# Filling the remainder of the MLP's gate and up contraction with zero rows to 128

## The chip, the cores and the metric

The kernel runs on one core of one Trainium2 chip, as one program. TensorE (PE in the profile, its weight loads apart as PEld) multiplies, VectorE (DVE), ScalarE (ACT) and GpSimd (POOL) do the elementwise work, and DMAs are issued from the queues of SyncE (SP) and ScalarE. The metric is the device time of one execution in microseconds (us); the time of a kernel is the median of several executions.

## The reference

One transformer block with adaptive layer norm: six modulation rows come from a conditioning vector, attention runs over a cached window of 512 keys, and a gated MLP follows. Sequence 2048, model width D = 576, 32 query and 16 key heads of 128, MLP width F = 4608, all float32.

```python
mod = (_silu(c) @ w_mod).reshape(c.shape[0], 6, 1, -1)
sa, ca, ga, sb, cb, gb = (mod[:, i] for i in range(6))
h = _layernorm(x) * (1 + ca) + sa
x = x + ga * _A_ref(h, A_k_cache, A_v_cache, A_wq, A_wo)   # attention
h = _layernorm(x) * (1 + cb) + sb
gate = jnp.einsum("bsd,df->bsf", h, W_gate)                # contraction over D = 576
up = jnp.einsum("bsd,df->bsf", h, W_up)                    # the same
gate = gate * (gate > 0)
x = x + gb * jnp.einsum("bsf,fd->bsd", gate * up, W_down)
```

## The kernel before

*Exact products from rounded parts.* Matrix operands are cut into a rounded high part and the difference as a low part (type float32r), and a product is high x high, low weight x high, and high weight x low: three matmuls that add up in one PSUM tile.

*The MLP's two contractions* (gate and up, side by side) are done as a Winograd form of Strassen's scheme: both operands are cut into 2 x 2 blocks, and seven products P1 to P7 of sums of blocks replace eight. The contraction of 576 is halved by this into 288 = 128 + 128 + 32. So one half has two full tiles of 128 rows (t = 0 and 1), each with a high and a low tile, and a remainder of 32 rows (t = 2). The remainder's three partial products are laid one above the other in the rows of one tile: the weights hold low, high, high in rows 0 to 95, the activations hold high, high, low. One matmul of 96 rows then does what three would. One product of one half (`prod`, line 967) is therefore seven matmuls: three for t = 0, three for t = 1, and the remainder at line 976. There are 36 steps m of seven products, gate and up each, so 504 products.

*Where the activations come from.* The layer norm of the MLP's input writes its transposed rows to DRAM (`hb_store`, line 240): four tiles of 128 rows for each block qb of 512 tokens, and a tile `hb[qb, 4]` of 2 x 3 x 32 rows, where each of the two halves' 32 remaining rows is stored three times. `hb_load` (line 250) reads them back. The sums of blocks that the products need (`B11`, `T2`, ...) are made by VectorE for the first half of the tokens (`h0_comb`, `h0_hi`, `h0_cut`, lines 844 to 874) and by GpSimd for the second (`h_later`, line 796, during the first half of the MLP), cut into high and low, and parked in DRAM tiles `hkeep` until `h_back` (line 877) loads them for the MLP half that uses them. In the profile these are the tiles h, hx, hy, hz, hk and hop.

*Where the weights come from.* In the first half (m = 0 to 17) raw tiles are loaded (`wr`), summed by VectorE (`w_sums`, line 783), and cut into `wop` by ScalarE and GpSimd (lines 753 to 755), and each `wop` is stored to DRAM (`wk`); the second half loads it from there. A raw weight tile has 128 rows for t = 2 already, four copies of its 32 rows.

*What sets the order.* TensorE, VectorE, ScalarE and GpSimd follow the order in which the code is written out: in attention a list of steps, each with a due time (`step(name, t, fn)`, t = 10 per unit of attention), in the MLP the slots of each product. Beside the products TensorE runs the down projection of the step before (`md`, line 632), which VectorE adds to the residual (line 643). SP's queue takes its DMAs in the order of the same code and holds at the first one whose buffer is not free. A DMA also waits for the transfer that last used its completion counter, of which there are eight.

Of the kernel before, what the change touches and what calls it, by code (L numbers as in the profile page):

```python
# [7 lines left out]
F32 = mybir.dt.float32  # L8
# [25 lines left out]
def kernel(  # L34
# [177 lines left out]
    def prep_out(d, k, src, key, slot=None, at=(None, "wC")):  # L212
# [11 lines left out]
        def cut():  # L224
# [9 lines left out]

    hT = [None] * NQB

    hb = {(qb, d): dr.tile([2, 3, 32, 512] if d == 4 else [P, 512], F32, name=f"hb{qb}_{d}")
          for qb in range(NQB) for d in range(5)}

    def hb_store(qb, d, cols, f, eng=None):  # L240
        eng = eng or nc.sync
        if d < 4:
            eng.dma_start(hb[qb, d][:, cols], f)
            return
        for j in range(2):
            s = f[32 * j:32 * j + 32]
            eng.dma_start(hb[qb, 4][j, :, :, cols].rearrange("r p n -> p r n"),
                              s[:, None, :].to_broadcast([32, 3, s.shape[1]]))

    def hb_load(dst, qb, j, t):  # L250
        if t < 2:
            nc.sync.dma_start(dst, hb[qb, 2 * j + t])
        else:
            nc.sync.dma_start(dst[:96], hb[qb, 4][j].rearrange("r p n -> (r p) n"))

    h0, late = {}, []
    pend, pend_act = [], []
# [516 lines left out]
    def w_sums(m, s):  # L774

        r = {ij: wraw.get((m, *ij)) for ij in RAW}
        if s == "S2":
# [8 lines left out]

    TERMS = {"B11": "+00", "B21": "+10", "T2": "+11-01+00", "T3": "+11-01", "T1": "+01-00",
             "T4": "+10-11+01-00", "B22": "+11"}
    hkeep = {(b, s, k): dr.tile([96 if k == 2 else P, 512], F32R, name=f"hk{b}_{s}_{k}")
             for b in range(2) for s in TERMS for k in range(5)}  # L790

    def terms_of(s, table):
# [3 lines left out]
    def h_later(b, s, t):  # L796

        st = {}
        n = 96 if t == 2 else P
        terms = terms_of(s, TERMS)  # L800

        def get(dst, j, k):
            hb_load(dst, 2 * b + k, j, t)

        def begin():
            if b:
                ab = wp.tile([P, 2, 512], F32, tag="wC", name=f"hx{b}_{s}_{t}")
                st["a"], st["b"] = ab[:, 0, :], ab[:, 1, :]
            else:
                for x in "ab":  # L810
                    st[x] = hp.tile([P, 512], F32, tag="hT", name=f"h{x}{b}_{s}_{t}")
            for x, term in zip("ab", terms):
                get(st[x], *term[1:])

        def comb(i):
            x, y = st["a"][:n], st["b"][:n]
            nc.gpsimd.tensor_tensor(x, x, y, op=ALU.add if terms[i][0] == "+" else ALU.subtract)
            if i + 1 < len(terms):
                get(st["b"], *terms[i + 1][1:])

        def cut():
            a = st["a"]
            hi = hp.tile([P, 512], F32R, tag="hT", name=f"hy{b}_{s}_{t}")
            nc.scalar.copy(hi[:n], a[:n])
            if t < 2:
                lo = st["b"].bitcast(F32R)
                nc.gpsimd.tensor_sub(lo, a, hi.bitcast(F32))
                stores.append((hkeep[b, s, 3 + t], lo))
            else:
                nc.gpsimd.tensor_sub(hi[64:96], a[64:96], hi[64:96].bitcast(F32))  # L830
            stores.append((hkeep[b, s, t], hi[:n]))

        return [begin] + [lambda i=i: comb(i) for i in range(1, len(terms))] + [cut]
# [8 lines left out]
        hb_load(h0[j, k, t], k, j, t)  # L842

    def h0_comb(dst, a, b, op, t):
        n = 96 if t == 2 else P
        nc.vector.tensor_tensor(h0[(*dst, t)][:n], h0[(*a, t)][:n], h0[(*b, t)][:n], op=op)

    hy0 = {}

    def h0_hi(s, x, t):  # L850
        a, n = h0[(*x, t)], 96 if t == 2 else P
        hi = hy0[s, t] = hp.tile([P, 512], F32R, tag="hT", name=f"hy0_{s}_{t}")
        nc.scalar.copy(hi[:n], a[:n])

# [4 lines left out]
            h0_cut(s, H0_CUT[s], t, True)  # L859

    def h0_cut(s, x, t, stay=False):
        a, n = h0[(*x, t)], 96 if t == 2 else P
        hi = hy0[s, t]
        if t < 2:
            lo = hy0[s, 3 + t] = hp.tile([P, 512], F32R, tag="hT", name=f"hz0_{s}_{t}")
            nc.gpsimd.tensor_sub(lo, a, hi.bitcast(F32))
        else:
            nc.vector.tensor_sub(hi[64:96], a[64:96], hi[64:96].bitcast(F32))
        if stay:
            if t == 2:  # L870
                hop[0, s] = [hy0[s, k] for k in range(5)]
            return
        if t < 2:
            stores.append((hkeep[0, s, 3 + t], lo))
        stores.append((hkeep[0, s, t], hi[:n]))

    def h_back(b, s):
        hs = hop[b, s] = [hp.tile([P, 512], F32R, tag="hT", name=f"hop{b}_{s}_{k}") for k in range(5)]
        for k in range(5):
            nc.sync.dma_start(hs[k][:96 if k == 2 else P].bitcast(F32), hkeep[b, s, k].bitcast(F32))  # L880


    WTERMS = {"P1": "+00", "P2": "+01", "P6": "+10+11-00", "P7": "+00-10", "P5": "+10+11", "P4": "+11",
# [83 lines left out]
    def prod(m, s, n, xx):  # L967
# [3 lines left out]
        ops = []  # L971
        for t in range(2):
            ops += [(w[:, xx, t, :], hs[t]), (w[:, xx, 3 + t, :], hs[t]), (w[:, xx, t, :], hs[3 + t])]
        ops.append((w[0:96, xx, 2, :], hs[2][0:96]))
        for i, (a, c) in enumerate(ops):
            nc.tensor.matmul(ps, a, c, start=s not in heir(m) and i == 0 and s not in seeds_of(m), stop=i == len(ops) - 1,  # L976
                             skip_group_check=True)
# [268 lines left out]
    def step(name, t, fn, *args):  # L1246
        sched.append((t + PLAN.get(name, 0), len(sched), fn, args))
# [151 lines left out]
    step("m3.col", 250, setd(mods, "b0", lambda: mod_col(3, 0.0)()))  # L1399
    step("m4.col", 400, setd(mods, "b", lambda: (mods["b0"], mod_col(4, 1.0)())))  # L1400

    mkeep = dr.tile([P, D], F32, name="mkeep")

    def m5_back():
# [317 lines left out]
```

## Time and profile before

| | us |
|---|---|
| median of three executions | 2897.92 (2895.86 to 2900.04) |
| the profiled execution | 2898.73 |
| its span, first to last instruction | 2895.9 |
| attention and what precedes it | 0 to about 1614 |
| first half of the MLP, with the weights' preparation | about 1614 to 2258 |
| second half of the MLP | about 2258 to 2896 |
| mean granted clock of TensorE in the span | 0.996 |

A line of a group reads: source line, engine, operation, output<-inputs by the program's names, shape and count, then busy time in us, mean duration of one in ns, and after the second bar the idle time of the engine just before them with what ended it. For a matmul, 128*128 or 96*128 are the rows and columns of the array that it uses. Matmuls overlap: each begins while the one before is still draining, so the distance between two starts says how long one holds the array, and its duration is longer than that. Lines of the timeline give start (us), duration (us) and the merged instructions; idle time before them stands in brackets.

### The profile page before, as it was taken

What the parts mean: (1) busy time and instruction counts of PE and PEld (TensorE: products, weight loads), DVE (VectorE), ACT (ScalarE), POOL (GpSimd) and SP (SyncE); (2) the same over time, 40 slices, a digit from 0 to 9 for tenths busy, and PEclk for the clock granted to TensorE, in tenths of its full rate; (3) what the DMA queues carried; (4) which work ended last, traced back from release to release, by engine and by line L of the source; (5) the groups of instructions that cost most, each with busy time, mean ns of one, the idle gap of its engine ahead of it and who ended that gap; (6) DMA issues with size and microseconds to landing.
All of it is one profiled execution on the core that took longest, in us unless ns stands there. A gap on an engine that the chain in (4) does not pass through costs nothing.

```text
span 2895.9 us, 41262 instructions
## 1 busy us (share of the span) xinstructions
PE 2852.8 (99%) x15214; PEld 2485.6 (86%) x15214; DVE 2145.8 (74%) x2967; ACT 1496.0 (52%) x2105; POOL 2115.4 (73%) x1564
## 2 busy tenths in 40 slices
PE   6999999999999999999999999999999999999999
PEld 5788888888888888888888888888888888888888
DVE  7778888888878888777889755676676466666666
ACT  5666666666676666666756444443444122222221
POOL 5688888888888889776778766777777256555553
PEclk9999999999999999999999999999999999999999
DMA  4012222222233223222244456666667954444442
GB/s 160 26 42 71 71 96 82 78 87 97 93 93 97 91 66 131 97 74 78 66 149 134 146 211 224 228 235 221 227 229 261 327 163 151 150 152 160 152 152 105
DMA packets 162697, 396.43 MB, mean 137 GB/s; under 512 B 14912, under 2 KB 61760, under 8 KB 162496
## 3 DMA queue, kind: packets, MB, share of 16 engines
q1 hardware_dynamic: 131472, 282.15, 30.4%
q10 hardware_dynamic: 31024, 111.65, 9.8%
q8 instruction: 120, 1.97, 0.3%
q14 instruction: 81, 0.66, 0.1%
HBM read 268.73 MB, written 153.32 MB: 146 GB/s over the span
## 4 chain that ended last, share of the span: by engine, by line
PE 91%; POOL 3%; DVE 3%; ACT 2%; issue 1%; DMA 1%; SPq 0%; ACTq 0%; POOLq 0%; DVEq 0%
PE gu L976 26%; PE wo L632 13%; PE qps L418 13%; PE md L632 8%; PE st_P L1078 6%; PE s L491 4%; PE s L490 4%; PE s L492 4%; PE pv L607 4%; PE pv L606 4%; PE pv L605 4%; PE qm L518 1%; POOL lo L572 1%; ACT p L565 0%; DVE ws L783 0%
## 5 line engine op out<-in xcount | busy, mean ns | idle before, releaser
L572 POOL TENSOR_TENSOR lo<-p,hi 128x1024 fp32r<-128x1024 f32 x256 | 608.8, 2401 | 1.1 <-ACT hi L552 1.1
L581 POOL TENSOR_TENSOR ks<-ks,p 128x512 f32<-128x512 f32 x256 | 343.7, 1342 | 270.5 <-ACT p L565 213.0
L495 DVE TRANSPOSE_TENSOR_REDUCE t<-s 128x32 f32<-128x1024 f32 x256 | 316.7, 1244 | 136.7 <-PE s L492 125.5
L976 PE MATMUL gu<-hop_B,wop 128*128 128x512 f32 (+1 forms) x1512 | 378.9, 394 | 0.1
L976 PEld LDWEIGHTS gu<-hop_B,wop 128*128 128x128 f32 (+1 forms) x1512 | 276.1, 188 | 52.7 <-ACT lflh L961 0.9
L976 PE MATMUL gu<-hop_T,wop 128*128 128x512 f32 (+1 forms) x1260 | 319.9, 393 | 0.0
L418 PE MATMUL qps<-hTa,wA 128*128 128x512 f32 x1288 | 311.2, 392 | 4.4 <-DVE hTa L366 2.1
L632 PE MATMUL wo<-woga,ohi 128*128 128x288 f32 x1472 | 306.7, 301 | 0.0
L563 DVE TENSOR_TENSOR p<-s,mb 128x1024 f32<-128x1024 f32 x246 | 290.3, 1219 | 4.1
L418 PEld LDWEIGHTS qps<-hTa,wA 128*128 128x128 f32 x1288 | 242.7, 189 | 57.4 <-DVE hTa L366 4.2
L552 ACT CAST hi<-p 128x1024 fp32r<-128x1024 f32 x256 | 269.2, 1052 | 7.1
L632 PE MATMUL md<-wogb,hhi 128*128 128x288 f32 x1280 | 262.2, 297 | 3.5 <-DVE acc L643 2.5
L565 ACT ACTIVATE p<-p 128x1024 f32<-128x1024 f32 x246 | 259.9, 1056 | 7.6 <-DVE p L563 7.4
L976 PEld LDWEIGHTS gu<-hop_T,wop 128*128 128x128 f32 (+1 forms) x1260 | 228.4, 188 | 41.0
L470 ACT ACTIVATE qhi<-qps 128x512 fp32r<-128x512 f32 x128 | 76.5, 597 | 340.4 <-PE qps L418 340.4
L643 DVE TENSOR_TENSOR acc<-md,acc 128x576 f32<-128x576 f32 x160 | 120.8, 755 | 169.3 <-PE md L632 168.9
L632 PEld LDWEIGHTS wo<-woga,ohi 128*128 128x128 f32 x1472 | 239.3, 189 | 7.3
L632 PEld LDWEIGHTS md<-wogb,hhi 128*128 128x128 f32 x1280 | 214.0, 189 | 16.6 <-DVE acc L643 4.0
L1087 DVE TENSOR_TENSOR acc<-st_P,acc 128x576 f32<-128x576 f32 x160 | 121.1, 757 | 133.8 <-PE st_P L1078 133.8
L632 PE MATMUL wo<-woga,olo 128*128 128x288 f32 x736 | 217.5, 295 | 0.4 <-POOL olo L621 0.3
L632 PE MATMUL md<-wogb,hlo 128*128 128x288 f32 x640 | 189.5, 296 | 0.0
L641 ACT COPY acc<-wo 128x576 f32<-128x576 f32 x233 | 148.2, 636 | 66.8 <-PE wo L632 61.6
(274 smaller groups left out, 7111.5 us busy)
## 6 DMA issues: line engine op xcount, KB each, us to landing
wop<-wk_P SPq DMA_DIRECT2D x133, 640.0 KB
wk_P<-wop ACTq DMA_DIRECT2D x119, 640.0 KB
wr<-wlay SPq DMA_DIRECT2D x68, 384.0 KB
rogb<-wd SPq DMA_DIRECT2D x68, 288.0 KB
againq<-akq SPq DMA_DIRECT2D x18, 640.0 KB
rwA<-wq SPq DMA_DIRECT2D x32, 320.0 KB
wlay<-wg SPq DMA_DIRECT2D x36, 256.0 KB
roga<-wo SPq DMA_DIRECT2D x32, 288.0 KB
```

Of the source, the lines that this page charges most:

```text
L418: return [lambda i=i, a=a, b=b: nc.tensor.matmul(ps, a, b, start=(i == 0), stop=(i == n - 1)) for i, (a, b) in enumerate(ops)]
L495: nc.vector.tensor_reduce(t4[u][:, 2 * h:2 * h + 2, :].rearrange("p k b -> p (k b)"), t.rearrange("p k (b j) -> p (k b) j", j=32), axis=AX ...
L552: nc.scalar.copy(hi_[u, h], pt[u, h])
L563: nc.vector.tensor_tensor(p, t, bc[u][:, None, :].to_broadcast([P, 2, 512]), op=ALU.subtract)
L565: nc.scalar.activation(p, p, AF.Exp, bias=0.0, scale=1.0)
L572: nc.gpsimd.tensor_sub(lo_[u, h], pt[u, h], hi_[u, h].bitcast(F32))
L581: nc.gpsimd.tensor_tensor(ks_[u], ks_[u], p[:, j, :], op=ALU.add)
L632: nc.tensor.matmul(ps[:, half, :H2], a[:, sl], w[b][:, cs], start=(n == 0 and seed is None), stop=(n == 5), skip_group_check=seed is not None)
L641: nc.scalar.copy(av, ps[:, :, :H2])
L976: nc.tensor.matmul(ps, a, c, start=s not in heir(m) and i == 0 and s not in seeds_of(m), stop=i == len(ops) - 1, skip_group_check=True)
L1078: nc.tensor.matmul(ps[:, j, :H2], x[:, sl], w[:, y, :], start=n == 0 and not second, stop=n == 2, skip_group_check=True)
L1087: nc.vector.tensor_tensor(t, ps[:, :, :H2], t, op=ALU.add)
```

## The change

The DRAM tile of the remainder gets a fourth row of blocks, `[2, 4, 32, 512]`, of zeros. A new step `hb.r` in attention (due at 300, before unit 30) fills it with eight DMAs of 32 x 512 from a part of `wmod` that the host has padded with zeros. Everything that touched 96 rows of the third activation tile now takes 128: its loads, the sums, the cast to the high part, the park in `hkeep`, and the reload; the subtraction that makes the low part stays on rows 64 to 95. The remainder's matmul uses all 128 rows of weights and activations; weight rows 96 to 127, a fourth copy of the high part, meet zeros.

```diff
-    hb = {(qb, d): dr.tile([2, 3, 32, 512] if d == 4 else [P, 512], F32, name=f"hb{qb}_{d}")
+    hb = {(qb, d): dr.tile([2, 4, 32, 512] if d == 4 else [P, 512], F32, name=f"hb{qb}_{d}")
...
-            eng.dma_start(hb[qb, 4][j, :, :, cols].rearrange("r p n -> p r n"),
+            eng.dma_start(hb[qb, 4][j, 0:3, :, cols].rearrange("r p n -> p r n"),
                               s[:, None, :].to_broadcast([32, 3, s.shape[1]]))
+
+    def hb_rest():
+        for qb in range(NQB):
+            for j in range(2):
+                nc.sync.dma_start(hb[qb, 4][j, 3], wmod[0, 64:96, 4 * D:4 * D + 512])
...
-            nc.sync.dma_start(dst[:96], hb[qb, 4][j].rearrange("r p n -> (r p) n"))
+            nc.sync.dma_start(dst, hb[qb, 4][j].rearrange("r p n -> (r p) n"))
...
-    hkeep = {(b, s, k): dr.tile([96 if k == 2 else P, 512], F32R, name=f"hk{b}_{s}_{k}")
+    hkeep = {(b, s, k): dr.tile([P, 512], F32R, name=f"hk{b}_{s}_{k}")
...
-        n = 96 if t == 2 else P
+        n = P
...
-            nc.sync.dma_start(hs[k][:96 if k == 2 else P].bitcast(F32), hkeep[b, s, k].bitcast(F32))
+            nc.sync.dma_start(hs[k].bitcast(F32), hkeep[b, s, k].bitcast(F32))
...
-        ops.append((w[0:96, xx, 2, :], hs[2][0:96]))
+        ops.append((w[:, xx, 2, :], hs[2]))
...
+    step("hb.r", 300, hb_rest)
```

The line `n = 96 if t == 2 else P` becomes `n = P` in `h_later`, `h0_comb`, `h0_hi` and `h0_cut` alike.

On SP's queue the eight new DMAs come into the attention phase, between the load of a tile of wq (`rwA`) and copies into the weights' DRAM layout (`wlay`); `wm` is a modulation tile, `rkv` keys. Before:

```order
L203 DMA rkv_0_4326<-kv 128x512
L1418 DMA wlay<-wu 2x128x256
L189 DMA rwA_4419<-wq 128x640
L1418 DMA wlay<-wu 2x128x256
L137 DMA wm_2_4544<-wmod 128x576
L1418 DMA wlay<-wg 2x128x256
```

With the change:

```order
L189 DMA rwA_4419<-wq 128x640
L253 DMA hb_4_142<-wmod 32x512 x2
L253 DMA hb_4_147<-wmod 32x512 x2
L253 DMA hb_4_152<-wmod 32x512 x2
L253 DMA hb_4_157<-wmod 32x512 x2
L1424 DMA wlay<-wu 2x128x256
L137 DMA wm_2_4552<-wmod 128x576
```

The copies and loads that followed `rwA` now stand behind eight more DMAs. Nothing else moves on this queue, and the other engines keep their order instruction by instruction.

Where the first half of the MLP hands over to the second, SP reloads the activations of the second half (`hop`, the third tile ends in `_2`) between the first weights of that half (`wop`). Before:

```order
L768 DMA wop_22812<-wk_P_159 128x1280
L880 DMA hop_T_0_22814<-hk_T_0_377 128x512
L880 DMA hop_T_1_22815<-hk_T_1_378 128x512
L880 DMA hop_T_2_22816<-hk_T_2_379 96x512
L880 DMA hop_T_3_22817<-hk_T_3_380 128x512
L880 DMA hop_T_4_22818<-hk_T_4_381 128x512
L768 DMA wop_22856<-wk_P_161 128x1280
```

With the change:

```order
L773 DMA wop_22820<-wk_P_159 128x1280
L885 DMA hop_T_0_22822<-hk_T_0_377 128x512
L885 DMA hop_T_1_22823<-hk_T_1_378 128x512
L885 DMA hop_T_2_22824<-hk_T_2_379 128x512
L885 DMA hop_T_3_22825<-hk_T_3_380 128x512
L885 DMA hop_T_4_22826<-hk_T_4_381 128x512
L773 DMA wop_22864<-wk_P_161 128x1280
```

The order is the same; each third tile carries 128 rows in place of 96.

More of the change, by code (lines that the diff above doesn't have):

```diff
@@ L844, in h0_comb @@
     def h0_comb(dst, a, b, op, t):
-        n = 96 if t == 2 else P
+        n = P
         nc.vector.tensor_tensor(h0[(*dst, t)][:n], h0[(*a, t)][:n], h0[(*b, t)][:n], op=op)
@@ L850, in h0_hi @@
     def h0_hi(s, x, t):
-        a, n = h0[(*x, t)], 96 if t == 2 else P
+        a, n = h0[(*x, t)], P
         hi = hy0[s, t] = hp.tile([P, 512], F32R, tag="hT", name=f"hy0_{s}_{t}")
@@ L861, in h0_cut @@
     def h0_cut(s, x, t, stay=False):
-        a, n = h0[(*x, t)], 96 if t == 2 else P
+        a, n = h0[(*x, t)], P
         hi = hy0[s, t]
```

## The prediction

> **What bounds the kernel now.** I read the page's busy shares first, then its chain of waits.
>
> ```profile
> span 2895.9 us, 41262 instructions
> PE 2852.8 (99%) x15214; PEld 2485.6 (86%) x15214; DVE 2145.8 (74%) x2967; ACT 1496.0 (52%) x2105; POOL 2115.4 (73%) x1564
> PE 91%; POOL 3%; DVE 3%; ACT 2%; issue 1%; DMA 1%; SPq 0%; ACTq 0%; POOLq 0%; DVEq 0%
> ```
>
> TensorE is the bound: 99% busy, and 91% of the chain. The other engines' time counts only where TensorE waits for it, so the next view is the MLP by stages (us, then busy us of PE, PEld, DVE, ACT and POOL, granted clock, DMA share, GB/s).
>
> ```profile
> 1614.00:2258.00 644.00, 641.37 (x3520) 565.20 (x3520) 418.82 (x408) 277.79 (x388) 474.10 (x411) 1.00 0.63 225
> 2258.00:2882.00 624.00, 622.95 (x3348) 545.03 (x3346) 394.44 (x547) 146.08 (x272) 338.69 (x331) 1.00 0.50 164
> 2240.00:2260.00 20.00, 20.00 (x112) 17.68 (x111) 10.03 (x9) 7.01 (x10) 13.06 (x11) 1.00 0.96 339
> 2260.00:2280.00 20.00, 19.93 (x110) 17.32 (x109) 8.94 (x12) 2.26 (x3) 2.57 (x2) 1.00 1.04 394
> 2280.00:2300.00 20.00, 20.00 (x109) 17.55 (x108) 10.51 (x15) 2.45 (x4) 3.90 (x3) 1.00 1.00 366
> ```
>
> In both halves TensorE has about 1 to 3 us of idle time to give back. So the change can gain only by making matmuls shorter, or by touching one of the few stalls. The DMA engines are half busy in general, but full from about 2240 to 2300, where the first half hands over to the second.
>
> **The matmuls that change.** One product is seven matmuls; its last is the 96-row remainder. The groups of that line, shapes kept apart (count, busy us, mean ns of one, idle before):
>
> ```profile
> L976 PE MATMUL gu<-hop_B,wop 128*128 128x512 f32 x1296 | 334.6, 393 | 0.1
> L976 PE MATMUL gu<-hz_T,wop 128*128 128x512 f32 x216 | 84.2, 390 | 0.0
> L976 PE MATMUL gu<-hop_B,wop 96*128 96x512 f32 x216 | 85.3, 395 | 0.0
> L976 PE MATMUL gu<-hop_T,wop 96*128 96x512 f32 x180 | 71.1, 395 | 0.0
> L976 PE MATMUL gu<-hy_T,wop 96*128 96x512 f32 x108 | 42.6, 395 | 0.0
> L976 PEld LDWEIGHTS gu<-hop_B,wop 128*128 128x128 f32 x1296 | 235.6, 188 | 43.7 <-ACT lflh L961 0.9 <-issue 0.5
> L976 PEld LDWEIGHTS gu<-hop_B,wop 96*128 96x128 f32 x216 | 40.6, 188 | 9.0
> ```
>
> There are 216 + 180 + 108 = 504 remainders. The weight loads are the same, 188 ns either way. The matmul itself is never shorter with fewer rows: 395 ns for 96, 390 to 393 for 128. So no work is added by the zero rows on TensorE, and there may be 2 to 5 ns to gain on each. Busy times overlap, so the bound on the gain is taken from the distances between starts (start us, duration us):
>
> ```profile
> 2001.15 0.39 PE L976 MATMUL gu<-hz_T,wop 128*128 128x512 f32 x1
> 2001.38 0.62 PE L976 MATMUL gu<-hy_T,wop 128*128 128x512 f32 x2
> 2001.84 0.39 PE L976 MATMUL gu<-hz_T,wop 128*128 128x512 f32 x1
> 2002.06 0.40 PE L976 MATMUL gu<-hy_T,wop 96*128 96x512 f32 x1
> 2002.29 0.43 PE L632 MATMUL md<-wogb,hhi 128*128 128x288 f32 x2
> ```
>
> A full-row matmul holds the array for 0.23 (2001.15 to 2001.38) or 0.22 us (2001.84 to 2002.06), the remainder for 0.23 (2002.06 to 2002.29). No gap of a whole switch is visible; what is there is at most 0.01 us, the grain of the view.
>
> *Term 1, 504 remainders at 128 rows.* Lower end 0 (0.23 against 0.23). Upper end 504 x 10 ns = 5.0 us of gain. No loss, since no full-row group of this line is above 395 ns. I take the mean of the two duration differences, 395 - 393 = 2 and 395 - 390 = 5, so 3.5 ns: **-1.8 us**.
>
> A rule speaks against even this. The Trainium skill, "TensorE: Matmul & The Clock Gate", section "Why this matters for your kernels", has a single matmul of K = 32 take the time of one with K = 128, so row count would be free in both directions. By that rule term 1 is 0 and the time is that of the first rival below. The trace agrees as far as 96 rows are no faster than 128; the extra 2 ns the rule leaves unexplained.
>
> *Term 2, casts, sums and subtractions on 128 instead of 96 rows.* The shapes stand side by side:
>
> ```profile
> L817 POOL TENSOR_TENSOR hx_T<-hx_T 128x512 f32<-128x512 f32 x14 | 18.0, 1285 | 1.7 <-DMA hx_T<-hb 1.5 <-DMA rogb<-wd 0.2
> L817 POOL TENSOR_TENSOR hx_T<-hx_T 96x512 f32<-96x512 f32 x7 | 9.0, 1285 | 2.2 <-DMA hx_T<-hb 2.2
> L824 ACT CAST hy_T<-hx_T 128x512 fp32r<-128x512 f32 x8 | 4.9, 618 | 2.5 <-POOL hx_T L817 2.5
> L824 ACT CAST hy_T<-hx_T 96x512 fp32r<-96x512 f32 x4 | 2.5, 618 | 1.8 <-POOL hx_T L817 1.7
> ```
>
> 1285 against 1285 ns, 618 against 618: rows cost nothing there. The four DVE sums of line 846 I put with them. **0 us**; even 5 ns on each of these 7 + 7 + 7 + 4 instructions would be 0.1 us.
>
> *Term 3, eight small DMAs on SP in the attention phase.* They stand between the load of a wq tile and the next weight copy on SP's queue:
>
> ```profile
> 414.52 0.33 SPq L189 DMA_DIRECT2D rwA<-wq  x1
> 414.89 0.58 SPq L1418 DMA_DIRECT2D wlay<-wu  x1
> 422.50 0.34 SPq L137 DMA_DIRECT2D wm<-wmod  x1
> ```
>
> At 0.33 to 0.58 us an issue, eight take 2.6 to 4.6 us. The copy at 414.89 behind them is not wanted before the MLP, and the next load that an engine waits for goes out at 422.50, after 7.0 us in which SP only waits. **0 us**; without that cover the wm load would be 4.6 us late, and DVE's modulation step after it.
>
> *Term 4, bytes.* Every transfer of the third tile grows from 192 to 256 KB: 18 loads (hx, h), 11 stores and 11 reloads (hk), 40 x 64 KB = 2.6 MB. At 63% DMA share this is hidden. In the full stretch it is not:
>
> ```profile
> 2245.86 4.39 SPq L880 DMA_DIRECT2D hop_B<-hk_B  x5
> 2254.62 3.91 SPq L768 DMA_DIRECT2D wop<-wk_P  x3
> 2260.43 5.28 PE L976 MATMUL gu<-hop_B,wop 128*128 128x512 f32 x21
> 2295.99 4.99 PE L976 MATMUL gu<-hop_B,wop 128*128 128x512 f32 x21
> ```
>
> Five reloads need 4.39 us to issue where one needs 0.33: SP is held by its own earlier transfers. Behind them stand the first wop loads of the second half, and 21 matmuls that begin at 2260.43 take 5.28 us where the same 21 take 4.99 later. So TensorE already waits some 0.3 us here, and the slack is nil. 64 KB (65.5 kB) at about 380 GB/s are 0.17 us; two enlarged reloads lie just ahead of that wop load (0.35 us), seven in the whole stretch (1.2 us). Lower end 0, if the extra rows travel beside the others; upper end 1.2 us. I take the middle, **+0.6 us**.
>
> Here too a rule differs. The Trainium skill, "SBUF — State Buffer", section "Door 1: The DMA port swizzle", puts partitions 96 to 127 on the same ports as 64 to 95, so a 96-row transfer leaves half of the ports half loaded, and the 32 rows would fill them for free. By it the term is 0 and the sum -1.8. No row here shows how long one 96-row load takes against one of 128.
>
> *Sum:* -1.8 + 0 + 0 + 0.6 = **-1.2 us**. The profiled execution took 2898.73 us (its span of 2895.9 and 2.8 around it), 0.8 above the median of 2897.92; so it would be 2897.5 there, and the median **2896.7 us**.
>
> **The rivals.**
>
> *TensorE gains nothing (0 ns on each remainder), the bytes stay:* 2897.92 + 0.6 = 2898.5 us. For it: the 0.23 against 0.23 us of the starts. Against it: three groups, 504 records, all at 395 ns.
>
> *Faster, because a stall goes.* There is one real stall in the MLP (idle time in brackets, then the chain around it):
>
> ```profile
> 2002.82 6.06 DVE L783 TENSOR_TENSOR wr<-wr,wr 128x768 f32<-128x768 f32 x1
> 2006.90:2009.60 2.70, 0.37 (x2) 0.00 (x0) 2.70 (x3) 0.00 (x0) 2.70 (x3) 1.00 1.00 401
> 2009.60 0.68 PE L632 MATMUL md<-wogb,hhi 128*128 128x288 f32 x2 [2.34 <-DVE acc L643]
> 2009.60 3.08 PE md L632 x12
> 2012.68 5.24 PE gu L976 x21
> 2017.92 1.60 PE md L632 x12
> 2048.39 4.83 PE gu L976 x21
> 2009.60:2013.20 3.60, 3.60 (x14) 3.50 (x15) 1.89 (x3) 1.45 (x2) 2.73 (x4) 0.53 0.62 211
> L783 DVE TENSOR_TENSOR wr<-wr,wr 128x768 f32<-128x768 f32 x17 | 21.2, 1248 | 0.0
> ```
>
> A DVE sum that means 1.25 us takes 6.06 while POOL, whose busy time is the fifth of the window's, has no break (2.70 of 2.70 us). The accumulation behind it (line 643) frees the PSUM tile late, TensorE idles 2.34 us, and then has a granted clock of 0.53 for 3.6 us: 3.08 - 1.60 + 5.24 - 4.83 = 1.9 us more. One such stall costs 4.2 us. It depends on which of DVE and POOL starts first, which a shift of a few tenths can turn. If it goes: -1.8 - 4.2 + 0.6 = -5.4, or 2892.5 us; with 5 ns on each remainder 2891.8, with the 10 ns bound 2889.3. Against it: nothing in the change is aimed there, and one in 68 such sums (four lists of 17) came out so.
>
> *Slower, by the same mechanism the other way.* The hx loads release POOL's combinations (line 817 waited for a DMA above), and 64 KB more in each moves POOL's row of work against DVE's sums. From the point where a sum is held over 3 us longer, TensorE idles and the clock drops, at 4.2 us each. Two stalls more than before: -1.8 + 0.6 + 8.4 = +7.2, or 2905.1 us. For it: DVE's four sums per step have little room in some steps, as 6.06 shows. Against it: 67 of 68 passed without harm, at the same durations on POOL.
>
> That the change does not do what it says can be left aside: the remainders' row count is in the instruction, and the profile will print it.
>
> **How the numbers follow.** The forecast, two small terms and as many stalls as before (2896.7): 0.46. TensorE gains nothing (2898.5): 0.18. A stall goes: 0.20; 0.14 of it are beyond the bound that follows, for which some 5 ns on a remainder must come with it (2891.8 to 2889.3), and 0.06 are not (2892.5). More stalls (2905.1): 0.16. About 0.2% of the median, 5.8 us, is what a measurement of this kernel can tell from no change, so faster means below 2892.1 and slower above 2903.7. Faster 0.14, within 0.2% 0.46 + 0.18 + 0.06 = 0.70, slower 0.16. The range for 8 times in 10 reaches from 2891.0, inside the case without the stall, to 2903.3, one stall more than before with the upper byte price and no gain on TensorE (2897.92 + 4.2 + 1.2).
>
> **What would show it.** The remainders appear as 128*128 with a mean of 390 to 393 ns in place of 395 (term 1; 395 again means the first rival). Lines 817 and 824 keep 1285 and 618 ns on 128 rows (term 2). The wm load still goes out near 422.5 us (term 3). The 21 matmuls near 2260 take more than 5.28 us (term 4; 5.28 or less means the rows travel for free). TensorE's waits list 2.3 us on line 643, none, or several of them: that decides between the rivals of both signs. The forecast is wrong if the first or the second MLP half differs by more than 3 us without such a wait.

## The result, and the profile after

The changed kernel takes 2884.07 us (median of six executions, 2881.82 to 2885.10), the kernel before beside it on the same chip 2896.15 (2894.11 to 2900.04). The ratio is 0.9956, with a 95% interval of 0.9943 to 0.9969: 12.1 us faster, and by the interval between 9.0 and 16.5. The forecast was 2896.7 with a range down to 2891.0, so the gain was put at a tenth of what it is. The profiled execution took 2884.48 us, its span 2882.7.

The page of the changed kernel, span and busy shares:

```profile
span 2882.7 us, 41271 instructions
PE 2839.4 (98%) x15214; PEld 2476.9 (86%) x15214; DVE 2149.1 (75%) x2967; ACT 1496.2 (52%) x2105; POOL 2115.0 (73%) x1564
```

TensorE ran the same 15214 matmuls in 13.4 us less busy time (2852.8 before) and its weight loads in 8.7 less (2485.6 before); no other engine's time moved by more than 3.3 us. So the time came out of the matmuls, not out of waits. The windows of the changed kernel by stage say where (columns as in the prediction):

```profile
1614.00:2258.00 644.00, 641.12 (x3545) 564.44 (x3543) 425.21 (x411) 280.00 (x391) 476.30 (x414) 1.00 0.64 231
2258.00:2882.00 624.00, 619.78 (x3396) 546.76 (x3396) 399.86 (x555) 144.37 (x269) 337.48 (x330) 1.00 0.48 166
2240.00:2260.00 20.00, 19.80 (x108) 17.13 (x107) 12.18 (x12) 5.73 (x8) 11.65 (x10) 1.00 0.99 372
2260.00:2280.00 20.00, 20.00 (x115) 17.82 (x114) 7.20 (x10) 2.26 (x3) 2.57 (x2) 1.00 1.04 406
2280.00:2300.00 20.00, 20.00 (x111) 17.65 (x110) 9.61 (x14) 3.46 (x5) 6.20 (x5) 1.00 0.92 333
2300.00:2850.00 550.00, 550.00 (x2994) 484.28 (x2994) 358.95 (x499) 136.20 (x257) 324.15 (x320) 1.00 0.46 155
```

The last stretch lies in the second half of the MLP and is the cleanest measure in this study, because nothing waits in it. The same stretch of the kernel before:

```profile
2300.00:2850.00 550.00, 550.00 (x2950) 481.12 (x2949) 353.50 (x491) 135.91 (x256) 322.75 (x319) 1.00 0.48 154
```

In both TensorE is busy for all of the 550 us, at a granted clock of 1.00. Before it gets 2950 matmuls through, after 2994: 44 more, 1.5%. 44 of 2994 in 550 us are 8.1 us. Nearly all products of this half are followed by six matmuls of its other work (`st_P`, 288 columns), 13 in all; 2994 / 13 = 230 products, so each with its six became 35 ns shorter. From the first matmul of a half to its last (the distance of two starts in the trace) the second half shrank by 8.9 us, from 614.1 to 605.2, and the first by 4.8, from 646.8 to 642.0.

The groups of the changed line in the changed kernel:

```profile
L981 PE MATMUL gu<-hop_B,wop 128*128 128x512 f32 x1512 | 374.5, 391 | 0.2 <-DMA wop<-wk_P 0.2
L981 PE MATMUL gu<-hop_T,wop 128*128 128x512 f32 x1260 | 316.0, 391 | 0.0
L981 PE MATMUL gu<-hy_T,wop 128*128 128x512 f32 x540 | 174.2, 392 | 0.2 <-POOL wop L760 0.2
L981 PE MATMUL gu<-hz_T,wop 128*128 128x512 f32 x216 | 84.8, 392 | 0.0
```

All 3528 matmuls are 128*128 now, at means of 391 to 392 ns; before they were 390 to 395. By the mean duration alone the change looks worth 3 to 4 ns on each remainder, as forecast. The starts tell more. Starts of neighbouring products in the second half, on TensorE's timeline of the kernel before:

```profile
2600.32 1.79 PE L976 MATMUL gu<-hop_B,wop 128*128 128x512 f32 x7
...
2602.75 1.79 PE L976 MATMUL gu<-hop_B,wop 128*128 128x512 f32 x7
```

And of the changed kernel:

```profile
2601.04 1.75 PE L981 MATMUL gu<-hop_T,wop 128*128 128x512 f32 x7
...
2603.43 1.76 PE L981 MATMUL gu<-hop_T,wop 128*128 128x512 f32 x7
```

One product and its six take 2.43 us before (2600.32 to 2602.75) and 2.39 after (2601.04 to 2603.43). That is 0.04 us, of which the remainder's own 3 to 4 ns are a small part. Where the rest sits is in the single records of TensorE: the mean distance in ns from each start to the next in this unit, by place, over the 223 products of the second half that six such matmuls follow.

| | 1st | 2nd | 3rd | 4th | 5th | 6th | 7th, the remainder | the six behind | in all |
|---|---|---|---|---|---|---|---|---|---|
| before | 234.7 | 230.8 | 235.4 | 228.2 | 232.0 | 230.6 | 232.5 | 806.8 | 2431.1 |
| changed | 232.4 | 230.7 | 226.7 | 226.7 | 226.7 | 226.7 | 226.7 | 796.4 | 2393.0 |

Of the 38 ns the remainder itself has 5.8, the six behind it 10, and the third to sixth matmul of the product 19, though these start nine to twelve places behind the last remainder.

The stall of the prediction's second rival did not go. On the changed kernel's timeline, VectorE's held sum and TensorE behind it:

```profile
2000.89 6.07 DVE L788 TENSOR_TENSOR wr<-wr,wr 128x768 f32<-128x768 f32 x1
...
2007.68 0.53 PE L637 MATMUL md<-wogb,hhi 128*128 128x288 f32 x2 [2.41 <-DVE acc L648]
...
2009.38 3.84 PE L981 MATMUL gu<-hop_B,wop 128*128 128x512 f32 x16
```

6.07 us for the sum and 2.41 us of idle TensorE, as before (6.06 and 2.34). Only the lowered clock behind it is missing this time: the twelve `md` matmuls take 1.70 us (2007.68 to 2009.38) where they took 3.08.

### The profile page after: what moved, and what is told of

Same layout as the page of the kernel before. It is cut to its first block, busy times and chain, and to the rows that moved or that the text cites. A ratio compares the mean times of both kernels' runs of the same rounds, so it can differ in the third digit from the quotient of the medians.

```text
span 2882.7 us, 41271 instructions
## 1 busy us (share of the span) xinstructions
PE 2839.4 (98%) x15214; PEld 2476.9 (86%) x15214; DVE 2149.1 (75%) x2967; ACT 1496.2 (52%) x2105; POOL 2115.0 (73%) x1564
## 4 chain that ended last, share of the span: by engine, by line
PE 90%; POOL 3%; DVE 2%; ACT 2%; DMA 2%; issue 1%; SPq 0%; ACTq 0%; POOLq 0%; DVEq 0%
PE gu L981 26%; PE wo L637 13%; PE qps L423 13%; PE md L637 8%; PE st_P L1083 6%; PE s L497 4%; PE s L496 4%; PE s L495 4%; PE pv L612 4%; PE pv L611 4%; PE pv L610 4%; PE qm L523 1%; POOL lo L577 1%; ACT p L570 0%; DVE ws L788 0%
## 5 line engine op out<-in xcount | busy, mean ns | idle before, releaser
L981 PE MATMUL gu<-hop_B,wop 128*128 128x512 f32 x1512 | 374.5, 391 | 0.2 <-DMA wop<-wk_P 0.2
L981 PEld LDWEIGHTS gu<-hop_B,wop 128*128 128x128 f32 x1512 | 275.0, 188 | 50.5 <-ACT lflh L966 0.9
L981 PE MATMUL gu<-hop_T,wop 128*128 128x512 f32 x1260 | 316.0, 391 | 0.0
L981 PEld LDWEIGHTS gu<-hop_T,wop 128*128 128x128 f32 x1260 | 227.8, 188 | 38.9
```

## The experiments

Eleven kernels, in the order of the questions. The table has the main figure of the first eight: matmuls in the busy stretch from 2300 to 2850 us, and the ratio of the time to that of the kernel before with its interval. The kernel before was measured again beside each: it took 2896.15 us beside the changed kernel, 2899.02 beside e1 to e4 and 2898.23 beside e5, e6, e9 and e10. So kernels are compared by their ratios rather than by their medians.

| kernel | rows of the seven matmuls | median us | ratio to before | matmuls in 550 us |
|---|---|---|---|---|
| before | 128 x 6, 96 | 2896.15 | | 2950 |
| changed | 128 x 7 | 2884.07 | 0.9956 (0.9943 to 0.9969) | 2994 |
| e1_mm96 | 128 x 6, 96, all data as changed | 2896.49 | 0.9994 (0.9985 to 1.0004) | 2947 |
| e4_copies | 128 x 7, copies for zeros | 2884.91 | 0.9955 (0.9938 to 0.9972) | 2991 |
| e3_all96 | 96 x 7 | 2889.40 | 0.9970 (0.9957 to 0.9983) | 2992 |
| e5_alt96 | 96 at places 2, 4 and 7 | 2897.92 | 0.9995 (0.9986 to 1.0005) | 2959 |
| e9_two96 | 96 at places 6 and 7 | 2896.11 | 0.9986 (0.9976 to 0.9996) | 2961 |
| e10_mid96 | remainder (96) at place 4 | 2896.20 | 0.9993 (0.9982 to 1.0004) | 2958 |
| e6_second96 | 96 in the second half alone | 2894.12 | 0.9984 (0.9975 to 0.9994) | 2949 |
| e2_mm64 | 128 x 6, 64 | 3078.43 | 1.0620 (1.0602 to 1.0638) | 2589 |

### Which part of the change brings it

*e1_mm96.* Everything of the change stays (zero rows, eight DMAs, larger transfers and sums), only the matmul goes back to 96 rows:

```diff
-        ops.append((w[:, xx, 2, :], hs[2]))
+        ops.append((w[0:96, xx, 2, :], hs[2][0:96]))
```

> The changed kernel with everything on 128 rows (zero rows, loads, sums, stores, reloads) except the remainder's matmul and its weight load, which go back to 96 rows. Theory A (the row count of the matmul costs the time: 504 x 24 ns = 12.1 us): it is as slow as the kernel before, 2896 us. Theory B (the transfers and sums on 128 rows brought the gain): it stays at 2884 us. My forecast's own terms (1.8 us from the matmul): 2886 us.

Measured: 2896.49 us, ratio 0.9994, the time of the kernel before. One line brings the whole gain, and the rest of the change costs and brings nothing that shows. The stretch from 2300 to 2850 agrees:

```profile
2300.00:2850.00 550.00, 550.00 (x2947) 480.98 (x2946) 353.11 (x490) 133.84 (x253) 322.27 (x318) 1.00 0.48 156
```

*e4_copies.* The fourth row of blocks is a fourth copy of the 32 rows in place of zeros, and the eight DMAs are gone. (The remainder's high x high product is counted twice in the output.)

```diff
-            eng.dma_start(hb[qb, 4][j, 0:3, :, cols].rearrange("r p n -> p r n"),
-                              s[:, None, :].to_broadcast([32, 3, s.shape[1]]))
+            eng.dma_start(hb[qb, 4][j, :, :, cols].rearrange("r p n -> p r n"),
+                              s[:, None, :].to_broadcast([32, 4, s.shape[1]]))
...
-    step("hb.r", 300, hb_rest)
```

> The changed kernel with the activations' 32 remainder rows stored a fourth time in place of the zeros, and without the eight DMAs that write the zeros; the product of the remainder's high parts is counted twice. If only the row count matters: 2884 us. If the zeros matter (less power, a higher granted clock): 2896 us. Theory B with the eight DMAs as a cost: below 2884 us by up to 1 us.

Measured: 2884.91 us, ratio 0.9955, as the changed kernel. That the rows are zeros plays no part, and the eight DMAs cost nothing that shows.

### Do 96 rows cost, or 96 among 128?

*e3_all96.* All seven matmuls of a product on 96 rows (rows 96 to 127 of the two full tiles are left out of the product):

```diff
         ops.append((w[:, xx, 2, :], hs[2]))
+        ops = [(a[0:96], c[0:96]) for a, c in ops]
```

> The changed kernel with all seven matmuls of a product on 96 rows; a quarter of the contraction of the full tiles is left out. Theory S (a change of row count between neighbouring matmuls costs, some 12 ns each): still two changes per product except where two products follow each other directly, so 2893 to 2896 us. Theory M (every matmul on 96 rows costs 24 ns): 2884 + 7 x 12.1 = 2969 us.

Measured: 2889.40 us, and 2992 matmuls in the stretch, two fewer than on 128 rows:

```profile
2300.00:2850.00 550.00, 550.00 (x2992) 484.30 (x2991) 357.79 (x498) 136.31 (x257) 325.76 (x321) 1.00 0.48 157
```

So a 96-row matmul is no slower than a full one: with seven times as many of them the loss in this stretch is gone. (In total it is 5.3 us above the changed kernel, with overlapping intervals. Of the 3.8 us between the two profiled spans 2.0 lie ahead of the first matmul of the MLP, where the kernels do the same.) Here the Trainium skill, "TensorE: Matmul & The Clock Gate", section "Why this matters for your kernels", gives a single matmul of K = 32 the time of one with K = 128. The trace agrees for 96 rows as long as all neighbours have 96 as well; no run here has 32. What the rule does not say is what a matmul among others of a different row count does to them.

*e5_alt96, e9_two96, e10_mid96.* Three, two, and one moved matmul on 96 rows, the others on 128 (rows 96 to 127 of the ones cut are left out in the first two):

```diff
+        ops = [(a[0:96], c[0:96]) if i in (1, 3, 6) else (a, c) for i, (a, c) in enumerate(ops)]
```

```diff
+        ops[5:] = [(a[0:96], c[0:96]) for a, c in ops[5:]]
```

```diff
-        ops.append((w[:, xx, 2, :], hs[2]))
+        ops.insert(3, (w[0:96, xx, 2, :], hs[2][0:96]))
```

> The changed kernel with the second, fourth and seventh matmul of each product on 96 rows, each between full-row ones; a quarter of the contraction of those two is left out. Theory I (each lone 96-row matmul among full-row ones costs 24 ns, a run of them costs next to nothing, as seven in a row did): 2884 + 3 x 12.1 = 2920 us. Theory O (the cost comes once per product): 2896 us.

> The changed kernel with the last two matmuls of each product on 96 rows (sixth and remainder); a quarter of the contraction of the sixth is left out. If the cost is in going to 96 rows and back, whatever the length of the run: 2896 us. If only a lone one costs: 2884 to 2889 us. If each costs: 2908 us.

> The changed kernel with the remainder on 96 rows as the fourth matmul of a product instead of the last. Theory I (a lone 96-row matmul costs wherever it stands): 2896 us. Theory P (it costs because the down projection's matmuls of 288 columns follow it): 2884 us for the products whose end is now full-row.

Measured: 2897.92, 2896.11 and 2896.20 us, within 0.2% of the kernel before (e9_two96 is 0.14% faster, clear of its interval), with 2958 to 2961 matmuls in the stretch. Where the kernel before passes 44 fewer than the changed one, these three pass 33 to 36 fewer. So in the second half three odd matmuls in a product cost no more than one, two side by side no more than one, and the odd one costs as a middle one too. The loss there is paid once per product in which row counts are mixed, whatever their number.

In the first half that does not hold. Between 1700 and 1980 us TensorE hardly waits in the kernel before, the changed kernel and e5_alt96 (in this order):

```profile
1700.00:1980.00 280.00, 279.86 (x1543) 246.17 (x1542) 178.28 (x176) 126.18 (x179) 201.87 (x180) 1.00 0.64 227
1700.00:1980.00 280.00, 279.97 (x1553) 246.41 (x1551) 181.71 (x178) 127.86 (x181) 203.45 (x182) 1.00 0.64 230
1700.00:1980.00 280.00, 280.00 (x1530) 245.23 (x1530) 170.79 (x174) 125.26 (x177) 200.60 (x179) 1.00 0.65 229
```

One odd matmul in each product loses 10 of 1553, three lose 23 (e9_two96 loses 13, e10_mid96 15). That e5_alt96 takes the time of the kernel before all the same is in part a coincidence: the stall on the accumulation is missing from its profiled execution, where TensorE does not wait once in the first half.

```profile
1614.00:2258.00 644.00, 644.00 (x3517) 565.45 (x3517) 409.20 (x408) 277.66 (x389) 472.07 (x412) 1.00 0.65 228
```

Whether the slower products took the stall away was not tested.

*e6_second96.* 96 rows in the second half of the MLP alone:

```diff
-        ops.append((w[:, xx, 2, :], hs[2]))
+        n2 = 96 if m >= NFP else P
+        ops.append((w[0:n2, xx, 2, :], hs[2][0:n2]))
```

> The changed kernel with the remainder on 96 rows in the second half of the MLP only. If every remainder costs the same 24 ns: half of 12.1 us, 2890 us. By the traces of before and after, where the first half is 4 us shorter and the second 9: 2893 us.

Measured: 2894.12 us, ratio 0.9984, where the changed kernel has 0.9956 and the kernel before 1. So the second half carries 0.28% or some 8 us, give or take 5, and the first the other 0.16% or 4.6 us (1.7 to 7.2). That fits the 8.9 and 4.8 us of the traces. Both halves have 252 remainders; this difference is taken up below.

*e2_mm64.* The remainder on 64 rows (one of its three partial products is left out):

```diff
-        ops.append((w[:, xx, 2, :], hs[2]))
+        ops.append((w[0:64, xx, 2, :], hs[2][0:64]))
```

> The changed kernel with the remainder's matmul on 64 rows; the product of the high weights and the low activations of the remainder is left out. Theory A1 (any count below 128 costs): 2896 us. Theory A2 (only three quarters of the array is bad): 2884 us.

Measured: 3078.43 us, 194 more than the changed kernel by the medians and 192 by the ratios, 380 to 386 ns for each of the 504 remainders. On TensorE's timeline:

```profile
2302.60 0.39 PE L981 MATMUL gu<-hz_T,wop 128*128 128x512 f32 x1
2302.92 1.15 PE L981 MATMUL gu<-hy_T,wop 64*128 64x512 f32 x3
...
2304.58 0.39 PE L981 MATMUL gu<-hz_T,wop 128*128 128x512 f32 x1
2304.90 0.50 PE L981 MATMUL gu<-hy_T,wop 64*128 64x512 f32 x1
2305.33 0.54 PE L637 MATMUL md<-wogb,hhi 128*128 128x288 f32 x2
```

The matmul ahead of the 64-row one holds the array for 0.32 us (2304.58 to 2304.90) in place of 0.23, the 64-row one itself for 0.43 (2304.90 to 2305.33). This is a switch that can be seen in the starts, and the next matmul waits for it. The Trainium skill, "TensorEngine Tiling (Array Packing)", section "Key Properties", has a change of tiling mode drain the engine; the trace agrees for 64 rows as far as there is a loss of the 0.1 and 0.2 us just read, but that it is a drain no row shows. With 96 rows no loss of this size is seen on any one matmul (at most 11 ns, in m2_forms below), so the 12 us are of another kind.

### The cost by itself

*m1_rows.* All else is taken away: products of seven matmuls from tiles that lie in SBUF, 40 products in each sequence. Nothing runs beside them but, at the start of a sequence, the copy of the one before out of PSUM (VectorE, 0.69 us) and its store.

```diff
+    for name, rows, small in SEQ:
+        t = ps.tile([P, 512], F32, tag="a", name=name)
...
+        for n in range(N):
+            for i, (a, c) in enumerate(OPS):
+                k = rows(n).get(i, P)
+                nc.tensor.matmul(t, w[0:k, a, :], hs[c][0:k], start=n == 0 and i == 0,
+                                 stop=n == N - 1 and i == 6, skip_group_check=True)
```

> All of the computation is left out but products of seven matmuls (128 columns by 512) from tiles that are loaded once: eleven sequences of 40 products, nothing else running beside them. Theory A, the mix of row counts itself costs TensorE time: with the remainder on 96 rows (sc) a product takes 25 to 35 ns more than with all on 128 (sb); in every second product (sd) half of that; with i = 1, 3, 6 (se) or i = 5, 6 (sf) on 96 rows the same 25 to 35 ns; with all seven on 96 (sg) nothing; with the remainder on 64 rows (sh) about 385 ns more. With six 288-column matmuls behind each product (sj against si) 25 to 45 ns, and sk equal to si. Theory B, the extra needs the rest of the kernel (transfers into SBUF, other engines' reads and writes): sc, sd, se and sf are within 5 ns of sb for each product, sj within 5 ns of si, while sh still costs some 385 ns.

One sequence is one PSUM tile, so the tile's own view has its length: durations in ns (min, median, max), then the first and the last start in us, then the forms (here in the proportion of 7).

```profile
L77 PE MATMUL sb<-h,w x280: 389/389/389, 73.8 to 137.1; 128*128 128x512 f32 x140
L77 PE MATMUL sc<-h,w x280: 389/393/399, 137.3 to 201.6; 128*128 128x512 f32 x120, 96*128 96x512 f32 x20
L77 PE MATMUL sd<-h,w x280: 389/389/399, 201.8 to 265.6; 128*128 128x512 f32 x140
L77 PE MATMUL se<-h,w x280: 393/395/401, 265.8 to 330.9; 128*128 128x512 f32 x80, 96*128 96x512 f32 x60
L77 PE MATMUL sg<-h,w x280: 389/389/393, 396.1 to 459.3; 96*128 96x512 f32 x140
L77 PE MATMUL sh<-h,w x280: 388/389/498, 459.5 to 538.5; 128*128 128x512 f32 x120, 64*128 64x512 f32 x20
```

From first to last start all-full products (sb) take 63.3 us, all on 96 rows (sg) 63.2, a 96-row remainder in each (sc) 64.3, in every second (sd) 63.8, three in each (se) 65.1, a 64-row remainder (sh) 79.0. One us over 40 products is 25 ns. From the single starts, leaving out each sequence's first and last product: 1586.7 ns for a full product, 1613.3 with a 96-row remainder, so **26.6 ns**, 1600.0 in every second product, 1633.3 with three, 1623.3 with two side by side, 1986.7 with 64 rows (the matmul ahead, the 64-row one and the next stand at 318, 428 and 333 ns against 226.7). With six 288-column matmuls behind each product, as `st_P` has it, 2386.7 (si) become 2406.7 with a 96-row remainder (sj, 20.0 ns) and 2400.3 with all seven on 96 (sk).

Theory A holds: no transfer, port or other engine is needed, the mix itself costs TensorE its time. Four of its numbers were off: three odd matmuls cost 46.6 and two side by side 36.6, not the same 25 to 35; a 96-row remainder with six 288-column matmuls behind it costs 20.0, not 25 to 45; and the all-96 product ahead of such six pays 13.6 by itself, not nothing. The second half of the MLP repeats neither the first nor the last of these: e5_alt96 passes 35 matmuls fewer there than the changed kernel, against 44 fewer in the kernel before, and e3_all96 two. The first half does repeat the higher price of three.

*m2_forms.* Is it the rows, or any change of form, and does it go by odd matmuls or by changes? As m1_rows, with

```diff
+    SEQ = [("ta", lambda n: {}), ("tb", lambda n: {}), ("tc", lambda n: {6: (96, 128, 512)}),
+           ("td", lambda n: {6: (128, 96, 512)}), ("te", lambda n: {6: (128, 128, 448)}),
+           ("tf", lambda n: {6: (112, 128, 512)}), ("tg", lambda n: {6: (127, 128, 512)}),
+           ("th", lambda n: {6: (96, 128, 512)} if n % 4 == 3 else {}),
+           ("ti", lambda n: {i: (96, 128, 512) for i in range(7)} if n % 2 else {}),
+           ("tj", lambda n: {i: (96, 128, 512) for i in range(7)} if n % 4 > 1 else {})]
```

where the three numbers are rows, output columns and moving columns.

> As m1_rows, without the rest of the computation: ten sequences of 40 products of seven matmuls from loaded tiles; only the form of some matmuls differs. Theory A, rows alone: what costs is a change in the number of rows (the partitions that the matmul contracts over). Then tc (remainder on 96 rows, as sc before) is 25 to 28 ns per product above tb (all full); tf (112 rows) and tg (127 rows) cost the same; td (all rows, 96 output columns) and te (all rows, 448 moving columns) cost nothing, te being shorter by 64/512 of 227 ns = 28 ns. Theory B, any change of form: td costs 25 to 28 ns as well, and te comes out near even with tb (28 ns saved, 26 paid). On distance, if one lone 96-row matmul costs some 26 ns whatever is around it: th (the remainder of every fourth product) 26 / 4 = 6.6 ns per product. If it is the change and not the matmul that costs, ti (every second product wholly on 96 rows: one change per product) costs 13 to 22 ns per product and tj (two products and two) half of ti; if only a lone odd matmul costs, ti and tj are within 3 ns of tb.

The same view of its tiles:

```profile
L77 PE MATMUL tb<-h,w x280: 389/389/389, 74.1 to 137.3; 128*128 128x512 f32 x140
L77 PE MATMUL tc<-h,w x280: 389/393/399, 137.5 to 201.8; 128*128 128x512 f32 x120, 96*128 96x512 f32 x20
L77 PE MATMUL td<-h,w x280: 387/392/399, 202.1 to 266.2; 128*128 128x512 f32 x120, 128*96 128x512 f32 x20
L77 PE MATMUL te<-h,w x280: 362/389/398, 266.5 to 329.5; 128*128 128x512 f32 x120, 128*128 128x448 f32 x20
L77 PE MATMUL tg<-h,w x280: 389/393/399, 394.2 to 458.5; 128*128 128x512 f32 x120, 127*128 127x512 f32 x20
L77 PE MATMUL ti<-h,w x280: 389/393/399, 522.5 to 586.8; 128*128 128x512 f32 x80, 96*128 96x512 f32 x60
L77 PE MATMUL tj<-h,w x280: 388/389/397, 587.0 to 650.8; 128*128 128x512 f32 x70, 96*128 96x512 f32 x70
```

63.2 us for the full products (tb); 64.3 with 96 rows, and just as much with 127 (tg). 96 output columns (td) cost 64.1 - 63.2 = 0.9 us over 40 products. A remainder of 448 moving columns (te) should save 64 / 512 of 227 ns, 28 ns a product, and saves 6.7 (1580.0 against 1586.7 ns from the single starts). So it is any of these changes of form, and theory A, rows alone, falls. In te all weight loads are alike (128x128), so a change in the weight load is not needed. On distance: th, the odd remainder in every fourth product, costs 6.3 ns a product, a quarter of 26.6; ti, with one change of row count per product and seven of a kind in between, costs as much as the lone odd matmul with its two changes (64.3 us, above the 13 to 22 ns that were expected of it), tj with half as many changes half of it (63.8). The mean distances between starts in ns, by place after the change, read from the single records:

| | at the change | next | 3rd | 4th | 5th | 6th | 7th |
|---|---|---|---|---|---|---|---|
| tb, no change | 226.7 | 226.7 | 226.7 | 226.7 | 226.7 | 226.7 | 226.7 |
| tc, one 96-row matmul, then six full | 232.3 | 237.7 | 232.3 | 231.0 | 226.7 | 226.7 | 226.7 |
| ti, seven of a kind, then seven of the other | 232.3 | 236.0 | 228.3 | 232.3 | 231.0 | 226.7 | 226.7 |

In these streams a change slows the matmul at which it happens and the three or four behind it, by 2 to 11 ns each and 26.6 together. A second change inside that time adds nothing of its own in tc, and little where there are many: in se, with six changes a product, all seven matmuls stand at 232 to 234. Each of m1_rows and m2_forms was executed once, on different chips; the products that both have (sb and tb, sc and tc) agree to 0.1 ns.

### A version that would beat both

*f1_sums_later.* The changed kernel, with VectorE's weight sums behind the accumulation of the same slot, so that a held sum (6.07 us above) does not delay it:

```diff
-                    sums(m, i)
+                    if i == 6:
+                        sums(m, i)
...
+                if (m or i) and not early and i != 6:
+                    sums(m, i)
```

> The changed kernel with one thing more: VectorE's weight sums (w_sums) of a slot come behind the accumulation of that slot's down projection, so that a sum held up by GpSimd no longer delays it. If the wait near 2005 us (2.4 us on the accumulation, and some 1.9 us of lowered clock after it) can be removed so: 2884.1 - 2.4 to 4.3 = 2880 to 2882 us, and TensorE's waits list no 2.4 us on line 648. If the held sum only delays something else (the casts of the weights, the next sums, the gating): no faster, 2883 to 2890 us, with a wait of some us on another line of the first half of the MLP.

Measured: 2895.21 us, ratio 0.9993 (0.9983 to 1.0003): the gain is lost, beyond both cases. TensorE's waits in its trace (line waited for, us in total, times, longest):

```profile
PE md L637 <- DVE acc L648: 4.0, 6, 1.3
PE gu L981 <- POOL wop L760: 3.5, 11, 0.6
```

The one wait of 2.4 us has become six of up to 1.3, and the cut weights now come late eleven times (0.2 us in all in the changed kernel). The second half is untouched (2993 matmuls in the stretch), so the loss lies in the first, whose window is

```profile
1614.00:2258.00 644.00, 636.20 (x3487) 554.48 (x3486) 431.43 (x405) 277.27 (x387) 472.15 (x410) 1.00 0.65 226
```

TensorE idles 7.8 us of it (644.00 - 636.20), 4.9 more than in the changed kernel, most of it in these two waits. That sums made later let the weights run late fits the rows, but no run tests it alone. The other half of the 10 us of span lies at the same waits: by the single records a product with a wait of 0.21 us in or behind it is 0.50 us longer than its kind, one with 1.29 us 1.58. So an interruption costs some 0.28 us beyond its idle time (0.16 of it is the overlap of two neighbours, each 0.39 us long and 0.23 after the other), and 19 such waits in place of three make some 4.5 us of it. No kernel of this study beats the changed one.

## Why the prediction was wrong

*Term 1, the remainders: right place and sign, but the wrong cost was counted, too small by a factor of seven.* The forecast was -1.8 us with -5.0 as the lower bound; measured is -12.1, or 24 ns for each of 504. The step that failed is "Upper end 504 x 10 ns = 5.0 us". It took the distance from the remainder's start to the next, found 0.23 us as for a full-row matmul, and left 10 ns for what the view could hide. So it priced a remainder by the remainder's own time alone, where the cost of a mixed form lies for the most part on other matmuls. Both halves of the comparison were inside the disturbance. A remainder stands at 232 ns instead of 227, which 0.01 us of grain hides; and of the 26.6 ns some 21 lie on the three matmuls behind it (in the second half of the kernel 32 of 38 lie on others), which the step never counted. The full-row neighbour that served as the yardstick (2001.15 to 2001.38, 0.23 us) was the third matmul behind a remainder, where the table of m2_forms still has 231 ns; the other one, at 0.22, was at the undisturbed pace. The same holds for the durations: 393 and 390 ns were means over disturbed and undisturbed matmuls (by place in a product of the first half they run from 389 to 399), where an undisturbed one has 389. Comparing 395 with 393 inside one kernel measures the difference between two disturbed kinds.

*The price by itself meets the total, but not the halves.* In the order of TensorE 119 of the 504 remainders are followed by the next product, the others by 288-column matmuls or transposes. 119 x 26.6 + 385 x 20.0 ns = 10.9 us, near 12.1 and inside the interval. But 12 of the 119 and 240 of the 385 are in the second half, which makes 5.1 us there and 5.7 in the first, and the traces have 8.9 and 4.8 (with the stall's clock in it), e6_second96 some 8 and 4.6. One half comes out too low and the other too high, so the sum agrees in part by luck. Why a product of the second half pays 35 to 38 ns in the kernel and 20 by itself is open. In both, part of it falls far behind the remainder: by itself (sj) the fourth to sixth matmul of a product stand at 236, 228 and 232 ns, against 226.7 without the odd one (si). The rule of four or five matmuls from m2_forms does not cover this. No run here changes the tiles or the order of those six.

*The rule against term 1* would have made it 0. For 96 rows it holds among equal neighbours (e3_all96, sg) and not for a mix.

*Term 2, casts and sums on 128 rows: right, 0.* The groups of the two lines in the changed kernel:

```profile
L822 POOL TENSOR_TENSOR hx_T<-hx_T 128x512 f32<-128x512 f32 x21 | 27.0, 1286 | 3.4 <-DMA hx_T<-hb 3.3
L829 ACT CAST hy_T<-hx_T 128x512 fp32r<-128x512 f32 x12 | 7.4, 617 | 3.7 <-POOL hx_T L822 3.6
```

1286 and 617 ns against 1285 and 618 (the four sums on VectorE took 1656 against 1642), and e1_mm96, with all of them on 128 rows, has the old time.

*Term 3, eight DMAs on SP: right in its result, the issue time undersized.* SP's queue in the changed kernel:

```profile
415.06 0.33 SPq L189 DMA_DIRECT2D rwA<-wq  x1
415.44 5.68 SPq L253 DMA_DIRECT2D hb<-wmod  x8
421.16 0.64 SPq L1424 DMA_DIRECT2D wlay<-wu  x1
423.04 0.33 SPq L137 DMA_DIRECT2D wm<-wmod  x1
```

They took 5.68 us, not 2.6 to 4.6, yet the wm load goes out at 423.04 (422.50 before): the 7 us in which SP only waited were the cover. Attention kept its time (1578.50 us of TensorE up to 1614, 1578.53 before).

*Term 4, bytes: at most a sixth of the +0.6 us.* At the handover the changed kernel's timeline has

```profile
2256.08 1.77 PE L981 MATMUL gu<-hop_B,wop 128*128 128x512 f32 x7
2258.04 3.42 PE L981 MATMUL gu<-hop_B,wop 128*128 128x512 f32 x14 [0.20 <-DMA wop<-wk_P]
```

The 21 matmuls that took 5.28 us end 5.38 us after their start, with a wait of 0.20 us on the weights. So the larger reloads may push a little, about 0.1 us; that the rows travel wholly free is not what this row shows, but e1_mm96 finds no cost in the total.

*The rivals.* That TensorE gains nothing falls with e1_mm96 against the changed kernel. The stall neither went nor multiplied (2.41 us against 2.34), so the gain is not the second rival's, though that one had the right sign. Such stalls do come and go, as it said: the profiled executions of e1_mm96 and e4_copies have two, that of e5_alt96 none. The "over 3 us" from which a held sum was to idle TensorE and drop the clock stands in no row: by the forecast's own 6.06, 1.25 and 2.34 us it is 2.5, and the drop doesn't always come. The half clock behind the stall was missing in this execution, 1.4 us on its twelve matmuls; the rest of the 13.2 us of span (2895.9 to 2882.7) is about term 1's 12.1. The forecast named its own failure: a half that differs by more than 3 us without a wait on the accumulation; both do, by 4.8 and 8.9.

## What to carry to other kernels

Where TensorE is the bound, keep the form of its matmuls (rows, output columns, moving columns) the same over long runs: fill a short contraction with zero rows to that of its neighbours if the rows cost nothing elsewhere, and group the odd forms together. Price such an edit by the length of the whole repeating unit, from one start to the same start in the next unit, or by the matmuls that pass in a stretch where TensorE is always busy. The odd instruction's own duration, and even its own start distance, show a fifth of it or less (5.6 of 26.6 ns by itself, 5.8 of 38 in the second half of this kernel).

## What the runs showed of the hardware

- Among equal matmuls of 512 columns a change of form costs TensorE 26.6 ns, spread over four or five of them, whether the rows become 96, 112 or 127 (tf is as long as tg in m2_forms, 64.3 us), and 21 to 23 ns where output or moving columns change (td 1610.0, te 1580.0 + 28 saved, against 1586.7). It was seen with no other engine at work. In a mix with 288-column matmuls the price differs (20.0 ns by itself, 38 in the second half of the kernel). What in TensorE does it stays open.
- 96 rows are as fast as 128 when all have 96 (63.2 and 63.3 us for 40 products).
- 64 rows among 128 are another matter: 380 to 386 ns for each switch there and back in the kernel, 400 ns by itself, visible as 0.32 and 0.43 us between starts.
